# A gated recurrence and a max-out layer on one core: a new opening order, weights folded in one fused step, transposes in halves

## The chip, the core and the metric

The kernel runs on one core of a Trainium2 chip. A core has five engines that run their own instruction queues in order: TensorE (PE: matmuls and the loads of their weights, PEld), VectorE (DVE), ScalarE (ACT), GpSimd (POOL), and SyncE (SP), which here only issues DMAs. The metric is the device time of one execution in microseconds (us); less is better.

## What is computed

A recurrence over time in each of 256 channels for 4 sequences of 6144 tokens, then a layer with the larger of two products:

```
sig = 1.0 / (1.0 + np.exp(-f_logit))
f = lower_bound + (1.0 - lower_bound) * sig
i = 1.0 - f
for t in range(S):
    h = f[:, t] * h + i[:, t] * x[:, t]
    y[:, t] = h
...
h1 = y @ w1            # 256 x 1024
h2 = y @ w2            # 256 x 1024
out = np.maximum(h1, h2) @ w_out     # 1024 x 256
```

The kernel writes 1 - lower_bound as `om` and uses three rewritings. With u = sigmoid(-f_logit), the forget term is f = 1 - om*u and the input term is om*u*x; the factor om is left out of the scan's input v = u*x and put into the weights instead. The maximum becomes h1 + relu(h2 - h1), so the hidden layer needs only the folded weight wd = om*(w2 - w1), and the linear part y @ w1 @ w_out is folded into one 256 x 256 matrix, `w13`.

## The kernel before, in words

The 24576 tokens are cut into 48 blocks of 512 (`TB`), 12 to a sequence. Channels lie on the partitions in two halves of 128 (`KC`), hidden units in 8 groups of 128 (`FC`). For each block PE does 8 slots: in a slot, one hidden group (`hidden`, L253: two matmuls of 512 columns into a PSUM buffer `dT`, of which there are five) and one eighth of the output product of the block before (`project`, L305: five matmuls of 256 columns into `psO`, three buffers). ScalarE turns each `dT` into `rt` by a relu (L234); 24 such buffers hold three blocks' worth.

The first four blocks (`NP`) are the opening. Their inputs are loaded in natural order as f32, gated by ScalarE (`gate_nat`, L107), multiplied by VectorE (`drive_nat`, L112), turned by PE through an identity matrix (`turn_pe`, L120), and scanned by VectorE (`scan`, L142). In the same stretch the weights are loaded in quarters of 256 hidden units ("chunks" 0 to 3; chunk k holds hidden groups 2k and 2k+1) and prepared: `diff` (L378) computes w2 - w1 in f32, `scale` (L384) multiplies by `om` into bf16 `wd`; `round_w1` and `round_wout` cast to bf16; `turn_w1`, `keep_w1`, `linear_weights` and `keep_linear` build `w13`.

What runs in which order in the opening is written out by hand in two strings. `LOADS` (L445) is the order of SP's loads: f0a is the first half of block 0's f_logit, x0a that of x, w13 is chunk 3 of w1, w23 chunk 3 of w2, wo3 chunk 3 of w_out. `PLAN` (L449) is the order of work; each engine takes its own items from it in that order. A suffix .a, .v or .p names ScalarE, VectorE or GpSimd. G is a gate, V a drive, TU and TV the turns of u and v, F a forget, S a scan, RW and RO casts of w1 and w_out, D a difference, SC a scaling, TW a turn of w1, KW its copy out of PSUM, W13 a piece of the linear weights, KL its copy out, H a hidden half or group, R a relu, P an output step (P020: block 0, hidden group 2, first 256 tokens), L a linear step, O a copy out, warm n idle matmuls. CA starts the feed of the later blocks.

From block 4 on, GpSimd casts f_logit and x of two blocks at a time (`cast`, L167) into a bf16 scratch in DRAM, and SP brings them into SBUF transposed (`turn_dma`, L176). `cast_behind` (L182) lets GpSimd read one element of a landed transpose before it issues the next pair's casts. `gate_of` and `turn_of` (L546 to L549) say in which slot a block is gated and a pair is turned; a gated block runs `gate`, `drive`, and for each half a forget and a scan (L579 to L585). Results are copied out of `psO` and sent by SP (`send_out`, L319) in groups of 256 rows, eight buffers deep.

Of the kernel before, what the change touches and what calls it, by code (L numbers as in the profile page):

```python
# [9 lines left out]
BF16 = mybir.dt.bfloat16  # L10
ALU = mybir.AluOpType
AF = mybir.ActivationFunctionType
P = 128
# [3 lines left out]
def kernel(  # L17
# [36 lines left out]
    scratch = ctx.enter_context(  # L54
        tc.tile_pool(name="scratch", bufs=1, space=bass.MemoryType.DRAM)
    )
    ttpool = ctx.enter_context(tc.tile_pool(name="turned", bufs=3))
    midpool = ctx.enter_context(tc.tile_pool(name="mid", bufs=2))
    ypool = ctx.enter_context(tc.tile_pool(name="ypool", bufs=4))
    rpool = ctx.enter_context(tc.tile_pool(name="rpool", bufs=3 * FC))  # L60
# [113 lines left out]
            )  # L174

    def turn_dma(c):  # L176
        for s, name in enumerate(("fs", "xs")):
            t = ttpool.tile([P, KC, CB * TB], BF16, name=("fT", "xT")[s])
            turned[c, s] = t
            nc.sync.dma_start_transpose(out=t[:], in_=spare[c % NS, name][:])  # L180

    def cast_behind(c):  # L182

        if c + 1 < NCH:
            last = CB * TB - 1
            nc.gpsimd.tensor_copy(out=held[:], in_=turned[c, 0][:, KC - 1, last : last + 1])  # L186
            cast(c + 1)

    def part(j, s):
        c, o = divmod(j - NP, CB)  # L190
        return turned[c, s][:, :, o * TB : (o + 1) * TB]

    def gate(j):
        ffs[j] = midpool.tile([P, KC, TB], BF16, name="ff")
        ys[j] = ypool.tile([P, KC, TB], BF16, name="y")
        us[j] = midpool.tile([P, KC, TB], BF16, name="u")
        nc.scalar.activation(out=us[j][:], in_=part(j, 0), func=AF.Sigmoid, scale=-1.0)  # L197

    def drive(j):
        vs[j] = midpool.tile([P, KC, TB], BF16, name="v")  # L200
        nc.vector.tensor_tensor(out=vs[j][:], in0=us[j][:], in1=part(j, 1), op=ALU.mult)  # L201

    def forget_half(j, h, on_act=False):
        forget(ffs[j][:, h, :], us[j][:, h, :], h, on_act)
# [107 lines left out]
    def copy_out(j, g, on_act=False):  # L312
# [3 lines left out]
        else:  # L316
            nc.vector.tensor_copy(out=osbs[j, g][:], in_=pos[j, g, 0][:])  # L317

    def send_out(j, g):  # L319
        r0 = j * TB + 2 * g * P  # L320
        nc.sync.dma_start(
            out=out[r0 : r0 + 2 * P, :].rearrange("(p r) d -> p r d", r=2),
            in_=osbs[j, g][:],
        )

    def store(j, g):
        copy_out(j, g)
# [47 lines left out]
        )  # L375
        nc.vector.tensor_scalar_add(out=nom[:], in0=pt, scalar1=-1.0)

    def diff(k, h, eng):  # L378
        cols = slice(k * QF, (k + 1) * QF)
        eng.tensor_tensor(  # L380
            out=wdf[:, h, cols], in0=w2n[:, h, cols], in1=w1n[:, h, cols], op=ALU.subtract
        )

    def scale(k, h, on_dve):  # L384
        cols = slice(k * QF, (k + 1) * QF)
        o, i, m = wd[:, h, cols], wdf[:, h, cols], om[:, h : h + 1]
        if on_dve:
            nc.vector.tensor_scalar_mul(out=o, in0=i, scalar1=m)  # L388
        else:
            nc.scalar.activation(out=o, in_=i, func=AF.Copy, scale=m)  # L390

    def turn_w1(k):
        pts[k] = ps_d.tile([P, 2, D], BF16, name="dT")
# [49 lines left out]


    LOADS = """  # L445
    f0a x0a f0b w13 w23 x0b w12 w22 wo3 w10 w20 w11 wo2 w21 f1a x1a wo0 f1b x1b wo1
    f2a f2b x2a x2b f3 x3
    """
    PLAN = """  # L449
    G0a RW3.p keeps_T keeps V0a TU0a D31.p warm3 TV0a D30.p G0b F0a0.v warm4 TU0b  # L450
    D21.p F0a1.v S0a1 S0a0 V0b F0b1.a warm1 TW3 F0b0.a RW0.p warm5 TV0b RW2.v S0b1
    D01.p KW3.a TW2 SC31.a SC30.a KW2.a S0b0 RO3.a H06a H07a D20.v SC21.a warm3 H06b
    SC20.v H07b D00.v W133 RW1.v R07.a TW0 H04b H04a RO2.p H05a R06.a P071 SC00.v
    H05b P070 P061 D10.p TW1 SC01.a KW0.v R05.a R04.v H01a KW1.v H00a H00b H01b P040
    P050 P060 G1a P041 SC10.v V1a W132 R01.a D11.p TU1a RO0.p SC11.a P051 TV1a R00.a
    H02a F1a1.v F1a0.a RO1.p H03b S1a1 P011 G1b H02b S1a0 P010 H03a R02.a W130 V1b
    P001 R03.a TU1b H17a F1b1.v P000 TV1b H15a F1b0.a S1b1 S1b0 G2a H16a P031 P030
    P021 G2b W131 KL1.v TU2a F2a0.a P020 H17b H15b KL0.v H16b L01 L11 R17.a TU2b
    H10a H10b R16.a V2a R15.v F2a1.v H11b O01.a P161 H11a TV2a F2b0.a H12b P151 L10
    P171 V2b H12a R11.a F2b1.v R10.a S2a1 TV2b S2a0 G3b P150 R12.a S2b1 G3a L00 S2b0  # L460
    H13a V3b TU3b O00.a H13b P101 R13.a F3b1.v H14a P160 F3b0.v H14b P100 P170 H20
    H26 V3a TU3a P111 F3a1.v H21 R14.a H27 R20.a F3a0.v R26.a TV3a S3a1 P120 H24
    TV3b R21.a P121 P110 S3a0 H22 R27.a S3b1 P130 R24.a R22.a S3b0 H23 P131 R23.a
    H25 P140 O10.v P141 R25.a O11.v CA
    """

    engines = {"a": nc.scalar, "v": nc.vector, "p": nc.gpsimd}
# [18 lines left out]
    def issue(item):  # L486
        name, _, e = item.partition(".")
        eng, on_dve, on_act = engines.get(e), e == "v", e == "a"
        kind = name.rstrip("0123456789ab")
        arg = ["ab".index(c) if c in "ab" else int(c) for c in name[len(kind) :]]  # L490
        if kind == "warm":
            keep_warm(arg[0])
        elif name == "keeps_T":
            turn_bound()
        elif name == "keeps":
            keeps()
        elif kind in ("G", "V") and len(arg) == 2:
            (gate_nat if kind == "G" else drive_nat)(arg[0], 2 * arg[1], 2 * arg[1] + 2)
        elif kind in ("TU", "TV"):
            turn_pe(arg[0], "UV".index(kind[1]), arg[1])  # L500
        elif kind == "F" and len(arg) == 3:
            j, x, h = arg
            tok = slice(x * HB, (x + 1) * HB)
            forget(ffs[j][:, h, tok], uT[j, x][:, h, :], h, on_act)
        elif kind == "S" and len(arg) == 3:
            j, x, h = arg
            scan(j, h, x * HB, (x + 1) * HB, vT[j, x][:, h, :])
        elif kind == "RW":
            round_w1(arg[0], eng)
        elif kind == "RO":  # L510
            round_wout(arg[0], eng)
        elif kind == "D":
            diff(arg[0], arg[1], eng)
        elif kind == "SC":
            scale(arg[0], arg[1], on_dve)
        elif kind == "TW":
            turn_w1(arg[0])
        elif kind == "KW":
            keep_w1(arg[0], eng)
        elif kind == "W":  # L520
            linear_weights(int(name[3]))
        elif kind == "KL":
            keep_linear(arg[0], on_dve)
        elif kind == "H":
            (hidden_half if len(arg) == 3 else hidden_whole)(*arg)
        elif kind == "R":
            relu(arg[0], arg[1], on_dve)
        elif kind == "P":
            pair_steps(arg[0], arg[2], [arg[1]])
        elif kind == "L":  # L530
            pair_steps(arg[0], arg[1], [FC, FC + 1])
        elif kind == "O":
            copy_out(arg[0], arg[1], on_act)
            outs.append(arg)
            send_pending()
        elif kind == "CA":
            nc.gpsimd.tensor_copy(out=held[:], in_=ins[2][1][:, 3, D - 1 : D])
            cast(0)
            turn_dma(0)
            cast_behind(0)  # L540
            send_pending()
        else:
            raise ValueError(item)
# [7 lines left out]
    with tc.manual_schedule():  # L551
        for j in range(NP):
            alloc_in(j)
        nc.scalar.dma_start(out=lbr[:], in_=lower_bound.rearrange("(h p) -> h p", p=P))
        for name in LOADS.split():
            load_item(name)
        nc.vector.memset(warm[:], 0.0)  # L557
        make_identity(nc, ident[:])
        nc.vector.tensor_copy(out=ident_b[:], in_=ident[:])
        keep_warm(7)  # L560
        for item in PLAN.split():
            issue(item)
        assert not outs

        for j in range(3, NBLK + 1):
            for fc in range(FC):
                if j < NBLK:
                    hidden(j, fc)
                project(j - 1, fc)
                if fc == 0 and j > 3:  # L570
                    store(j - 2, 1)
                if fc == 4 and j < NBLK:
                    store(j - 1, 0)
                if j == NBLK and fc in (3, 5, 7):
                    if fc == 3:
                        store(j - 1, 0)
                    else:
                        store_row(j - 1, 1, (fc - 5) // 2)
                if (j, fc) in gate_of:  # L579
                    b = gate_of[j, fc]  # L580
                    gate(b)
                    drive(b)
                    for h in range(KC):
                        forget_half(b, h)
                        scan_half(b, h)  # L585
                if (j, fc) in turn_of:
                    turn_dma(turn_of[j, fc])
                    cast_behind(turn_of[j, fc])
# [30 lines left out]
```

## Time and profile before

| | |
|---|---|
| median of 7 runs | 397.62 us (397.07 to 397.79) |
| the profiled execution | 397.61 us, its span 395.8 us |
| mean granted TensorE clock | 0.999 |
| PE busy from 0 to 10 us | 8.17 of 10.00 us |
| PE busy from 10 to 20 us | 9.28 of 10.00 us |
| PE busy from 20 to 30 us | 10.00 of 10.00 us |
| PE busy from 100 to 200 us | 99.32 of 100.00 us |
| HBM over the span | 257 GB/s |

The span is the time from the first to the last instruction of the program in the profile; the execution's time has a little around it (397.61 against 395.8). A busy share is the time in which an engine works on at least one instruction. Some matmul records are missing from the trace, which shows as a small loss in busy time where there is none. Warm-up matmuls, whose results nobody reads, count as busy too, so a busy PE in the first 14 us isn't a useful PE.

Other rows of the profile that the opening touches, with shapes kept apart over the first 36 us (out<-in, shape, count, busy us, mean ns of one): the gate of 512 elements on ScalarE takes 626 ns, a forget of 256 elements 473 ns on ScalarE and 345 ns on VectorE, a scan of 256 elements 732 ns on VectorE, a relu of 512 elements 595 ns on ScalarE, a scaling of 256 elements 507 ns on ScalarE. In the steady part a gate of 1024 elements takes 1048 ns, a scan of 512 elements 1284 ns, a copy out of `psO` 679 ns.

### The profile page before, as it was taken

The page shows a single profiled execution, that of the slowest core. Times are in us where ns is not written, and L with a number is a line of the kernel's source. Part 1 is how long each engine was busy: PE and PEld are TensorE (multiplying, and loading weights), DVE is VectorE, ACT ScalarE, POOL GpSimd, SP SyncE. Part 2 cuts the span into 40 slices and gives each one's busy share as a digit, 9 for nine tenths or more (in the row PEclk, how much of TensorE's full clock was granted, in tenths as well). Part 3 has the DMA queues.
Part 4 walks back from the last instruction along what each step waited for, and adds up shares of the span by engine and source line. Part 5 has one row for each costly group of instructions (what it writes and reads, how often), then busy time and mean ns, then how long its engine had stood idle before and what let it go on. Part 6 is the DMA issues. An engine that isn't in the chain of part 4 may idle for free.

```text
span 395.8 us, 7146 instructions
## 1 busy us (share of the span) xinstructions
PE 387.8 (98%) x2793; PEld 275.0 (69%) x2840; DVE 251.8 (64%) x366; ACT 273.7 (69%) x451; POOL 36.9 (9%) x83
## 2 busy tenths in 40 slices
PE   8999999999999999999999999999999999999996
PEld 3796677777676777776767777767677777676775
DVE  3896965656755775576567656755775576567622
ACT  4787776677667666766676677667766766676661
POOL 2411011101101101101101001011011010100000
PEclk9999999999999999999999999999999999999999
DMA  7999999999999999999989999998998898981122
GB/s 241 350 247 186 237 213 214 235 218 215 237 199 196 236 207 222 193 228 201 209 193 196 198 206 198 221 216 184 205 208 208 186 192 206 214 188 53 55 81 107
DMA packets 125079, 79.12 MB, mean 200 GB/s; under 512 B 94195, under 2 KB 101621, under 8 KB 125045
## 3 DMA queue, kind: packets, MB, share of 16 engines
q1 hardware_dynamic: 113072, 55.59, 57.3%
q0 software_dynamic: 11968, 23.07, 35.4%
q8 instruction: 22, 0.36, 0.4%
q14 instruction: 13, 0.10, 0.1%
q10 hardware_dynamic: 4, 0.00, 0.0%
HBM read 53.48 MB, written 48.23 MB: 257 GB/s over the span
## 4 chain that ended last, share of the span: by engine, by line
PE 95%; DMA 1%; DVE 1%; issue 1%; SPq 1%; DVEq 0%
PE psO L268 53%; PE dT L245 39%; PE dT L225 2%; DMA xn<-in_x_dram 1%; PE dT L126 1%; SPq L100 0%; PE psO L413 0%; DVE vn L113 0%; SPq L344 0%; DVE y L149 0%; DVE wdf L380 0%; DVE wd L388 0%; DVE row L332 0%; PE dT L396 0%; DVEq L113 0%
## 5 line engine op out<-in xcount | busy, mean ns | idle before, releaser
L240 ACT ACTIVATE rt<-dT 128x512 bf16<-128x512 f32 x382 | 223.5, 596 | 106.4 <-PE dT L245 102.9
L268 PE MATMUL psO<-wob,rt 128*128 128x256 bf16 x1536 | 231.0, 273 | 0.2
L268 PEld LDWEIGHTS <-rt 128*128 128x128 bf16 x1536 | 150.0, 98 | 94.6
L245 PE MATMUL dT<-y,wd 128*128 128x512 bf16 x690 | 208.8, 379 | 2.2
L149 DVE TENSOR_TENSOR_SCAN y<-ff,y,v 128x512 bf16<-128x512 bf16 x82 | 105.3, 1284 | 2.9
L317 DVE COPY osb<-psO 128x512 f32<-128x512 f32 x93 | 62.8, 679 | 68.2 <-PE psO L268 68.2
L245 PEld LDWEIGHTS <-wd 128*128 128x128 bf16 x736 | 72.0, 98 | 8.8
L268 PE MATMUL psO<-w,y 128*128 128x256 bf16 x384 | 72.4, 273 | 0.0
L201 DVE TENSOR_TENSOR v<-u,xT 128x1024 bf16<-128x1024 bf16 x44 | 30.5, 693 | 59.6 <-ACT u L197 53.0
L197 ACT ACTIVATE u<-fT 128x1024 bf16<-128x1024 bf16 x44 | 46.1, 1048 | 0.5 <-DMA fT<-fs 0.5
L268 PEld LDWEIGHTS <-y 128*128 128x128 bf16 x384 | 37.6, 98 | 4.4
L186 POOL CAST held<-fT 128x1 f32<-128x1 bf16 x21 | 4.6, 218 | 280.7 <-DMA fT<-fs 280.7
L138 DVE TENSOR_SCALAR ff<-u,nom 128x512 bf16<-128x512 bf16 x88 | 29.8, 338 | 0.0
L170 POOL DMA_DIRECT2D fs<-in_f_logit_dram x22 | 12.3, 560 | 5.1 <-issue 5.0
L170 POOL DMA_DIRECT2D xs<-in_x_dram x22 | 12.1, 551 | 0.0
L149 DVE TENSOR_TENSOR_SCAN y<-nff,y,dT 128x256 bf16<-128x256 bf16 x14 | 9.6, 732 | 1.8 <-PE dT L126 1.3
L225 PE MATMUL dT<-y,wd 128*128 128x256 bf16 x64 | 10.1, 273 | 0.3 <-DVE wd L388 0.2
L433 PE MATMUL psO<-warm 128*128 128x512 bf16 x22 | 7.9, 493 | 1.2 <-DVE warm L557 1.2
L149 DVE TENSOR_TENSOR_SCAN y<-ff,v 128x512 bf16<-128x512 bf16 x6 | 7.3, 1225 | 0.2
L108 ACT ACTIVATE un<-fn 128x512 bf16<-128x512 f32 x8 | 4.9, 626 | 3.2 <-DMA fn<-in_f_logit_dram 3.1
L113 DVE TENSOR_TENSOR vn<-un,xn 128x512 bf16<-128x512 bf16 x8 | 6.1, 766 | 1.2 <-DMA xn<-in_x_dram 1.2
L225 PEld LDWEIGHTS <-wd 128*128 128x128 bf16 x64 | 5.8, 98 | 1.4 <-DVE wd L388 0.4
(40 smaller groups left out, 52.1 us busy)
## 6 DMA issues: line engine op xcount, KB each, us to landing
out_dram<-osb SPq DMA_DIRECT2D x95, 256.0 KB, 3.1
fs<-in_f_logit_dram POOLq DMA_DIRECT2D x22, 512.0 KB, 6.8
xs<-in_x_dram POOLq DMA_DIRECT2D x22, 512.0 KB, 9.5
fn<-in_f_logit_dram SPq DMA_DIRECT2D x6, 256.0 KB, 6.0
xn<-in_x_dram SPq DMA_DIRECT2D x6, 256.0 KB, 5.8
w1n<-in_moe_w_dram SPq DMA_DIRECT2D x4, 256.0 KB, 6.0
w2n<-in_moe_w_dram SPq DMA_DIRECT2D x4, 256.0 KB, 6.0
won<-in_moe_w_out_dram SPq DMA_DIRECT2D x4, 256.0 KB, 6.0
```

Source lines behind the costliest of these rows:

```text
L113: nc.vector.tensor_tensor(out=vs[j][:, q0:q1, :], in0=us[j][:, q0:q1, :], in1=ins[j][1][:, q0:q1, :], op=ALU.mult,)
L138: nc.vector.tensor_scalar(out=o, in0=i, scalar1=nom[:, h : h + 1], scalar2=1.0, op0=ALU.mult, op1=ALU.add)
L149: nc.vector.tensor_tensor_scan(out=ys[j][:, h, t0:t1], data0=ffs[j][:, h, t0:t1], data1=v, initial=initial, op0=ALU.mult, op1=ALU.add,)
L170: nc.gpsimd.dma_start(out=spare[c % NS, name][:], in_=src[b, k * TB : (k + CB) * TB, :], max_dma_last_dim=4096,)
L197: nc.scalar.activation(out=us[j][:], in_=part(j, 0), func=AF.Sigmoid, scale=-1.0)
L201: nc.vector.tensor_tensor(out=vs[j][:], in0=us[j][:], in1=part(j, 1), op=ALU.mult)
L225: nc.tensor.matmul(dts[j, fc][:, tok], lhsT=wd[:, kc, unit(fc)], rhs=ys[j][:, kc, tok], start=(first and kc == 0), stop=(not first and kc ...
L240: nc.scalar.activation(out=rt[:], in_=dts[j, fc][:], func=AF.Relu)
L245: nc.tensor.matmul(dts[j, fc][:], lhsT=wd[:, kc, unit(fc)], rhs=ys[j][:, kc, :], start=(kc == 0), stop=(kc == KC - 1),)
L268: nc.tensor.matmul(ps, lhsT=lhsT, rhs=rhs, start=start, stop=stop, skip_group_check=True)
L317: nc.vector.tensor_copy(out=osbs[j, g][:], in_=pos[j, g, 0][:])
L433: nc.tensor.matmul(idle[:].rearrange("p r d -> p (r d)"), lhsT=warm[:, 0:P], rhs=warm[:], start=True, stop=True,)
```

## The change

It has five parts.

1. The weights are folded in another form. `diff` and `scale` go; `fold_w1` (plan item A) computes om*w1 into `wdf` on GpSimd, ScalarE or VectorE, and `fold_diff` (item B) computes om*w2 - wdf on VectorE in one operation. Before, there were 8 differences and 8 scalings; after, 8 A (6 on GpSimd, one each on ScalarE and VectorE) and 8 B.
2. `LOADS` and `PLAN` are new. Block 0's x moves ahead of the weights, chunk 1 is the first to be used (H03, H02), then chunks 3, 2 and 0. The warm matmuls are 26 in place of 23.
3. `CA` waits for an element of block 2's f_logit in place of its x; with the new load order that is the load before.
4. `turn_dma` issues four transposes of one block each (f, x, f, x) in place of two of two blocks; the buffers are twice as many and half as large. `send_out` sends blocks 45 and 46 in two halves of a group each.
5. In the loop a gated block does both forgets before the drive; block 4's forgets go to ScalarE.

The diff, without what only follows from names:

```diff
-    ttpool = ctx.enter_context(tc.tile_pool(name="turned", bufs=3))
+    ttpool = ctx.enter_context(tc.tile_pool(name="turned", bufs=6))
...
     def turn_dma(c):
-        for s, name in enumerate(("fs", "xs")):
-            t = ttpool.tile([P, KC, CB * TB], BF16, name=("fT", "xT")[s])
-            turned[c, s] = t
-            nc.sync.dma_start_transpose(out=t[:], in_=spare[c % NS, name][:])
+        b0, n = NP + c * CB, CB
+        for o in range(n):
+            for s, name in enumerate(("fs", "xs")):
+                t = ttpool.tile([P, KC, TB], BF16, name=("fT", "xT")[s])
+                turned[b0 + o, s] = t
+                nc.sync.dma_start_transpose(
+                    out=t[:], in_=spare[c % NS, name][o * TB : (o + 1) * TB, :]
+                )
...
-            last = CB * TB - 1
-            nc.gpsimd.tensor_copy(out=held[:], in_=turned[c, 0][:, KC - 1, last : last + 1])
+            b0, n = NP + c * CB, CB
+            nc.gpsimd.tensor_copy(out=held[:], in_=turned[b0, n - 1][:, KC - 1, TB - 1 : TB])
             cast(c + 1)
...
     def send_out(j, g):
+        if NBLK - 4 < j < NBLK - 1:
+            for r in range(2):
+                nc.sync.dma_start(out=rows_out(j, g)[:, r, :], in_=osbs[j, g][:, r, :])
+        else:
+            nc.sync.dma_start(out=rows_out(j, g), in_=osbs[j, g][:])
...
-    def diff(k, h, eng):
-        eng.tensor_tensor(
-            out=wdf[:, h, cols], in0=w2n[:, h, cols], in1=w1n[:, h, cols], op=ALU.subtract
-        )
+    def fold_w1(k, h, eng):
+        o, i, m = wdf[:, h, cols], w1n[:, h, cols], om[:, h : h + 1]
+        if eng is nc.scalar:
+            nc.scalar.activation(out=o, in_=i, func=AF.Copy, scale=m)
+        else:
+            eng.tensor_scalar_mul(out=o, in0=i, scalar1=m)
...
-    def scale(k, h, on_dve):
-        o, i, m = wd[:, h, cols], wdf[:, h, cols], om[:, h : h + 1]
-        if on_dve:
-            nc.vector.tensor_scalar_mul(out=o, in0=i, scalar1=m)
-        else:
-            nc.scalar.activation(out=o, in_=i, func=AF.Copy, scale=m)
+    def fold_diff(k, h):
+        nc.vector.scalar_tensor_tensor(
+            out=wd[:, h, cols],
+            in0=w2n[:, h, cols],
+            scalar=om[:, h : h + 1],
+            in1=wdf[:, h, cols],
+            op0=ALU.mult,
+            op1=ALU.subtract,
+        )
...
     LOADS = """
-    f0a x0a f0b w13 w23 x0b w12 w22 wo3 w10 w20 w11 wo2 w21 f1a x1a wo0 f1b x1b wo1
-    f2a f2b x2a x2b f3 x3
+    f0a x0a f0b x0b w12 w11 w13 w21 wo1 w23 w22 wo3 f1a w10 w20 x1a f1b wo2 x1b wo0
+    f2a x2a f2b x2b f3 x3
     """
     PLAN = """
-    G0a RW3.p keeps_T keeps V0a TU0a D31.p warm3 TV0a D30.p G0b F0a0.v warm4 TU0b
-    D21.p F0a1.v S0a1 S0a0 V0b F0b1.a warm1 TW3 F0b0.a RW0.p warm5 TV0b RW2.v S0b1
-    D01.p KW3.a TW2 SC31.a SC30.a KW2.a S0b0 RO3.a H06a H07a D20.v SC21.a warm3 H06b
-    SC20.v H07b D00.v W133 RW1.v R07.a TW0 H04b H04a RO2.p H05a R06.a P071 SC00.v
+    G0a V0a keeps_T TU0a warm1 TV0a keeps A20.p F0a1.a S0a1 G0b RW1.p F0a0.a warm7
+    TU0b V0b F0b0.a S0a0 A11.p warm2 TV0b F0b1.a RW2.a A31.p A10.a S0b0 S0b1 B10 B11
+    warm4 TW2 TW1 RW3.a KW1.a warm2 TW3 RO1.a A21.v A30.p warm3 H03a H02a H03b B31
+    B30 KW2.a KW3.v B21 B20 H02b RO3.p W131 H06a R02.a H06b A00.p R06.v R03.a RW0.v
+    H07a P020 P021 H07b G1a W133 H05a H05b R07.a P061 A01.p H04a R05.a H04b B00 TW0
+    TU1a RO2.p B01 V1a P070 P030 H00a R04.a F1a1.v H01b H01a KW0.a TV1a P031 P060
...
         elif kind == "CA":
-            nc.gpsimd.tensor_copy(out=held[:], in_=ins[2][1][:, 3, D - 1 : D])
+            nc.gpsimd.tensor_copy(out=held[:], in_=ins[2][0][:, 3, D - 1 : D])
...
                     gate(b)
+                    for h in range(KC):
+                        forget_half(b, h, b == NP)
                     drive(b)
                     for h in range(KC):
-                        forget_half(b, h)
                         scan_half(b, h)
```

## The prediction

> **What bounds the kernel now.** I read the page's busy shares first, then the chain that ended last, then the chain in order of time over the first 45 us, SP's issues, and last the groups of the opening with shapes kept apart.
>
> ```profile
> PE 387.8 (98%) x2793; PEld 275.0 (69%) x2840; DVE 251.8 (64%) x366; ACT 273.7 (69%) x451; POOL 36.9 (9%) x83
> PE 95%; DMA 1%; DVE 1%; issue 1%; SPq 1%; DVEq 0%
> ```
>
> PE is busy 98% of the span and 95% of the chain. The chain in order of time (start, length, what) shows where the other 5% lie:
>
> ```profile
> 3.28 5.68 DMA xn<-in_x_dram
> ...
> 9.06 1.21 DVE vn L113
> ...
> 12.20 0.75 DVE wdf L380
> ...
> 12.97 0.72 DVE wd L388
> ...
> 13.74 0.83 PE dT L225 x6
> ...
> 41.78 0.55 PE psO L268 x5
> 42.33 0.43 PE dT L245 x2
> 42.76 0.55 PE psO L268 x5
> ```
>
> Until 13.74 us the chain runs over a load and VectorE; from 13.74 it is PE alone. From 41.78 a slot (two 128x512 and five 128x256 matmuls) takes 42.76 - 41.78 = 0.978 us, so a block of 8 slots takes 7.82 us; the same row stands at 374.13 us, 340 slots of 0.9775 later. So there is nothing to win or lose between 13.74 us and the end unless a new stall is made; the kernel's time is PE's useful work plus what PE loses before 13.74.
>
> That loss is a ledger. Useful matmuls before 13.74: 28 transposes at 0.054 us (four take 0.22 in the chain) = 1.5, and 12 of 256 columns at 0.109 = 1.3. Lost: 13.74 - 2.8 = 10.9 us. The rest is warm-up matmuls and waits.
>
> SP has eight DMA semaphores in turn, so from load 11 on it issues load n+8 when load n has landed (start, length):
>
> ```profile
> 6.28 0.43 SPq L344 DMA_DIRECT2D w2n<-in_moe_w_dram  x1
> 7.53 0.37 SPq L344 DMA_DIRECT2D w1n<-in_moe_w_dram  x1
> 8.25 0.37 SPq L349 DMA_DIRECT2D won<-in_moe_w_out_dram  x1
> 8.98 0.37 SPq L344 DMA_DIRECT2D w2n<-in_moe_w_dram  x1
> 9.75 0.37 SPq L100 DMA_DIRECT2D fn<-in_f_logit_dram  x1
> 10.50 0.37 SPq L100 DMA_DIRECT2D xn<-in_x_dram  x1
> 11.25 0.37 SPq L349 DMA_DIRECT2D won<-in_moe_w_out_dram  x1
> 12.01 0.37 SPq L100 DMA_DIRECT2D fn<-in_f_logit_dram  x1
> ```
>
> These are landings of places 3 to 10: 6.28, 7.53, 8.25, 8.98, 9.75, 10.50, 11.25, 12.01, then one each 0.75 us. All these loads are 256 KB, so I keep the places and put the new order into them.
>
> ```profile
> L380 POOL TENSOR_TENSOR wdf<-w2n,w1n 128x256 f32<-128x256 f32 x6 | 4.3, 726 | 1.3 <-DMA w2n<-in_moe_w_dram 1.2
> L388 DVE TENSOR_SCALAR wd<-wdf,om 128x256 bf16<-128x256 f32 x3 | 2.0, 652 | 0.0
> L355 POOL CAST w1b<-w1n 128x512 bf16<-128x512 f32 x2 | 1.2, 614 | 7.0 <-DMA w1n<-in_moe_w_dram 7.0
> ```
>
> The second number is the mean of one in ns: prices of the operations that go or that resemble the new ones.
>
> **What the skill says.** SBUF — State Buffer, section Who interferes with whom: a VectorE operation with two SBUF inputs, or in a two-port mode, and a GpSimd operation that reads SBUF exclude each other for the whole instruction. The trace agrees: L388 took 0.46 us on one occasion and 0.72 and 0.78 beside GpSimd work; the drive product (L113) took 0.68 alone, and 1.20 when it began at 9.06 with GpSimd's L380 running to 9.72. GPSIMD Engine Reference, section 3.1: 2.6 cycles per element with two inputs, 1.03 for short bodies bound by one port. The trace fits: 256 elements with two inputs 0.726 us, a 512-element cast 0.614. TensorE: Matmul & The Clock Gate, Part 1: the array starts at half rate and is freed after about 3.4 us of work. Here warm-up matmuls are 0.43 us apart until about 6.2 us and 0.217 after.
>
> **The change, part by part.**
>
> *Weight folding.* Before, a 256-column half cost a difference (0.726 on GpSimd, 0.41 undisturbed on VectorE), which needs w1 and w2, then a scaling. Now A = om*w1 needs w1 alone and is ready early; after w2 lands only B is left, one fused VectorE operation with two f32 SBUF inputs. The trace shows neither. B: nearest row VectorE's L380, 0.41 us, 0.34 start to start; bounds 0.38 and 0.55; I take 0.41. A on GpSimd: the cast leaves 0.614 - 512*1.03/1200 = 0.17 fixed, so 0.17 + 256*1.03/1200 = 0.39 below; above, the two-input 0.73; I take 0.45.
>
> *New load order*, by place: x0b 4 (7.53), w12 5, w11 6 (8.98), w13 7 (9.75), w21 8 (10.50), wo1 9 (11.25), w23 10 (12.01), w22 11 (12.76), wo3 12 (13.51), w10 14, w20 15 (15.8).
>
> *The walk to the first hidden matmul (H03a).* VectorE, in its order: V0b at 7.57 takes 0.68, then three scans (0.73 each, 0.66 to 0.73 apart): y of block 0 complete at 10.3. Then B10 at 10.52 (w21 plus a signal), B11 at 10.86, done 11.30. GpSimd has A11 done near 10.1 (after RW1, 9.01 to 9.62), ScalarE A10 at 9.84: both ready. PE meanwhile: TW3 waits for ScalarE's cast of w13 (9.77 to 10.40), then three warm matmuls, 10.66 to 11.31. Both chains meet: H03a at 11.33. Useful by then: the 28 transposes, 1.5. Lost: 9.8.
>
> *After it.* H03, H02 in halves (4 x 0.217) and W131 (0.43) fill PE to 12.65. H06a needs B31 and B30, which start at 12.05 when w23 is there and end at 12.79: hole 0.2. Then H06, H07a, P020, P021, H07b fill to 14.15. W133 needs wo3's cast on GpSimd: lands 13.51, GpSimd waits for B20's port to 13.83, cast done 14.34: hole 0.24. Chunk 0 (w20 at 15.8) is wanted at about 16.8 and ready then. Later the two engines that feed PE have no queue longer than its stock. Lost in all 9.8 + 0.2 + 0.24 + 0.05 small ones = 10.3, against 10.9: **gain 0.6 us**.
>
> *Cast gate.* The first casts wait for f2b at place 23 instead of x2b at 24: about 0.75 us sooner. They meet the last loads f3, x3: up to about 1 us later, and G3a stands early in ScalarE's queue (about 25.1 against a landing of 24.6). Relus behind it have half a microsecond or more of stock. I take 0; a wait over 1.5 us would cost up to 0.9.
>
> *Block 4's forget on ScalarE.* Before, its gate ran from 38.46 (1.05 us), its VectorE work ended at 43.38, its first use was at 44.1. Now two 512-wide activations, 0.47 + 256*0.83/1000 = 0.69 each, run beside the drive, and VectorE loses 0.68. ScalarE is late by 1.05 + 1.3 = 2.3 us; relus take 0.60 of each 0.978 slot and five dT buffers hold some 3.9 us. No stall; without that cover about 1 us.
>
> *Transposes halved* (88 for 44 on SP, order f, x, f, x), turned buffers doubled. The next cast now waits for the x of the pair's first block: the second index of `turned` is the stream. Cycle: cast to landing of xs 9.5 (the median), half a transpose about 1.0 to 1.7 and 2.2 to land, 0.5 of issue: 13.2 to 13.9 us, against 13.2 to 14.3 between the issues of casts 3 to 6 (50.64, 64.89, 78.35, 91.59 us) and 15.64 that PE takes for two blocks. From block 12 on f has landed at least 5 us before its gate (90.77 against 96.13), so 0; SP's outs behind a transpose have eight buffers.
>
> *Outputs of blocks 45, 46 in two*: four more SP issues of 0.33 us at a time when SP waits; the last output stays where it was. *Forgets before the drive*: same VectorE sum. Both 0.
>
> Sum against the profiled execution, 397.61 us (span 395.8): 397.0. The median is 397.62, so no correction.
>
> **Rivals.** *Larger gain*: the two holes and the start all hang on landings of w21, w23, wo3. Should these come 0.25 us earlier, the start and both holes shrink: gain 1.1, 396.5. For it: places are a steady 0.75 us apart. Against: the bytes ahead of them are the same. *No gain*: y of block 0 ends only 0.2 us before B10. If x0b takes 0.4 us longer in place 4 (place 3 was 2.1 us after place 2, which I can't explain), or the clock stays half past 8.5 us so that the seven warm matmuls hold TU0b back, H03a comes 0.5 later: 397.5. *Slower, by GpSimd*: A11, A31, A30 stand behind one another, and B waits for each as well as for its port. At 0.45 they end at 11.0 with a microsecond to spare; each 0.1 us above about 0.55 moves start and H06a together. Break-even is near 0.8 us, above the two-input row; at 1.0 us H03a begins 0.6 later and H06a's hole and chunk 0 lose as much again: 398.8. For it: a pointer scalar in software is unpriced. Against: one stream should not cost more than two. *Starved feed*: halved transposes costing as much as whole ones, and casts slowed with them, past 15.64 us a pair; each 0.3 us over, times 20 pairs, is 6 us: about 403.
>
> **How the numbers follow.** A measurement of this kernel tells about 0.2%, 0.8 us, from no change. Forecast near 397.0 (396.8 to 397.4): 0.50, no measurable change. Larger gain 0.24: faster. No gain 0.10: within. GpSimd 0.10 and feed 0.06: slower. So faster 0.24, within 0.60, slower 0.16. The range leaves out the feed, half of the GpSimd case and the largest gains: 396.3 to 398.2.
>
> **What would show it.** The first L225 row near 11.3, a wait of 0.2 before the next pair of L225, a L424 matmul waiting for GpSimd's wob near 14.4, then PE alone at 0.978 a slot; block 4 with no gap. Wrong: A on GpSimd over 0.6 us, B over 0.5, y of block 0 after 10.5, or any PE gap past 20 us.

## The result, and the profile after

| | before | after |
|---|---|---|
| median of all runs shown | 397.48 us (396.54 to 398.08, 31 runs) | 402.2 us (397.86 to 406.65, 13 runs) |
| ratio after : before | | 1.0096, interval 1.0076 to 1.0115 |
| span of the profiled execution | 395.8 us | 400.4 us |
| mean cycle from one pair's casts to the next, from the second casts on | 15.11 us | 15.95 us |

The changed kernel is slower by about 1%. Its runs also spread over 9 us, those of the kernel before over 1.5 us. The ratio leaves out the runs that lie more than 1.5% above the fastest; for this kernel they showed the same TensorE clock as the others, so the spread is its own, and the ratio of the plain medians (402.2 / 397.48 = 1.012) is as fair a number.

The page of the changed kernel: busy shares, shares of the chain that ended last, the row of DMA load (tenths, 40 slices), groups (busy us, mean ns | idle before, released by), and the DMA issues with their median us to landing. The two rows of the kernel before that they are compared with follow.

```profile
PE 390.6 (98%) x2796; PEld 274.2 (68%) x2843; DVE 247.3 (62%) x363; ACT 272.5 (68%) x456; POOL 44.0 (11%) x81
DMA  7999999989999999989999999999999999999523
PE 67%; DMA 24%; ACT 4%; issue 2%; DVE 2%; SPq 1%; POOL 1%; ACTq 0%; POOLq 0%; DVEq 0%
L197 ACT ACTIVATE u<-fT 128x1024 bf16<-128x1024 bf16 x44 | 46.3, 1052 | 31.1 <-DMA fT<-fs 31.0
L201 DVE TENSOR_TENSOR v<-u,xT 128x1024 bf16<-128x1024 bf16 x44 | 30.3, 688 | 17.6 <-DMA xT<-xs 15.6
fs<-in_f_logit_dram POOLq DMA_DIRECT2D x22, 512.0 KB, 7.7
xs<-in_x_dram POOLq DMA_DIRECT2D x22, 512.0 KB, 11.0
```

```profile
L197 ACT ACTIVATE u<-fT 128x1024 bf16<-128x1024 bf16 x44 | 46.1, 1048 | 0.5 <-DMA fT<-fs 0.5
xs<-in_x_dram POOLq DMA_DIRECT2D x22, 512.0 KB, 9.5
```

PE's share of busy time is 98% as before and tells nothing. The chain does: PE holds 67% of it where it held 95%, and DMA 24% where it held 1%. The gates of the steady part (L197) waited 31.0 us for the transposed f_logit; in the kernel before they waited 0.5 us. The second cast of a pair (xs) lands 11.0 us after its issue, before 9.5.

Where the time goes is read from the first output step of each block (my own reading of PE's timeline). Block 3's stands at 44.35 us (before 44.55), block 20's at 177.29 (before 177.49): in this pair of traces the opening won 0.2 us, and 17 blocks later nothing was lost. Block 24's stands at 210.41 (before 208.77), and PE ends at 397.29 (before 392.73). The loss is 4.77 us in stretches near 178, 195, 211, 259, 306, 322 and 339 us. The first of them in the chain in order of time (start, length, what):

```profile
172.57 0.42 PE psO L268 x4
172.99 4.25 DMA fT<-fs
...
177.35 1.06 ACT u L197
178.41 1.47 ACT rt L240 x3
...
179.92 0.50 PE psO L268 x3
```

The transpose of the pair's first f lands late, the gate starts late at 177.35, three relus stand behind it in ScalarE's queue, and PE waits for the last of them. The forecast of 397.0, no change, was wrong; what came resembles its "starved feed" rival (about 403), to which it gave 0.06.

Around this stretch, SP's transposes and GpSimd's casts in the changed kernel, and then SP's transposes of the same pair in the kernel before (start, length of the issue, what, and in brackets the idle time before):

```profile
172.99 1.23 SPq L182 DMA_TRANSPOSE fT<-fs  x1
176.22 1.23 SPq L182 DMA_TRANSPOSE xT<-xs  x1
177.54 1.25 SPq L182 DMA_TRANSPOSE fT<-fs  x1
178.84 1.29 SPq L182 DMA_TRANSPOSE xT<-xs  x1
```

```profile
162.51 0.64 POOL L190 CAST held<-xT 128x1 f32<-128x1 bf16 x1 [14.13 <-DMA xT<-xs]
163.08 0.55 POOL L170 DMA_DIRECT2D fs<-in_f_logit_dram  x1
163.62 0.55 POOL L170 DMA_DIRECT2D xs<-in_x_dram  x1
179.73 0.64 POOL L190 CAST held<-xT 128x1 f32<-128x1 bf16 x1 [15.55 <-DMA xT<-xs]
180.30 0.55 POOL L170 DMA_DIRECT2D fs<-in_f_logit_dram  x1
```

```profile
158.93 3.84 SPq L180 DMA_TRANSPOSE fT<-fs  x1
162.85 2.12 SPq L180 DMA_TRANSPOSE xT<-xs  x1
```

In the changed kernel fs of this pair landed at 172.94, and SP issued the first f at once. It was done issuing at 174.22, and the second f, whose data were there, could have followed. But SP issues in order, and the next in the queue was the first x, which waits for xs: that landed at 176.16. So the second f went out at 177.54, 3.3 us later than its data allowed. It and the second x were then still to be moved when the next casts went out at 180.30. From casts to casts this pair took 17.2 us; PE uses a pair up in 15.64. So what comes late is the next pair, its first f with it: all the gates that waited were those of the first block of a pair.

### The profile page after: what moved, and what is told of

The parts are those of the page before. It is cut to its first block, busy times and chain, and to the rows that moved or that the text cites. A ratio compares the mean times of both kernels' runs of the same rounds, so it can differ in the third digit from the quotient of the medians.

```text
span 400.4 us, 7198 instructions
## 1 busy us (share of the span) xinstructions
PE 390.6 (98%) x2796; PEld 274.2 (68%) x2843; DVE 247.3 (62%) x363; ACT 272.5 (68%) x456; POOL 44.0 (11%) x81
## 4 chain that ended last, share of the span: by engine, by line
PE 67%; DMA 24%; ACT 4%; issue 2%; DVE 2%; SPq 1%; POOL 1%; ACTq 0%; POOLq 0%; DVEq 0%
PE psO L268 38%; PE dT L245 28%; DMA fT<-fs 9%; DMA xs<-in_x_dram 8%; ACT rt L240 3%; DMA xT<-xs 3%; ACT u L197 2%; DMA fn<-in_f_logit_dram 2%; DMA w2n<-in_moe_w_dram 1%; DMA w1n<-in_moe_w_dram 1%; DVE y L149 1%; SPq L100 0%; POOL fs L170 0%; DVE v L201 0%; DVE osb L317 0%
## 5 line engine op out<-in xcount | busy, mean ns | idle before, releaser
L240 ACT ACTIVATE rt<-dT 128x512 bf16<-128x512 f32 x379 | 215.7, 596 | 83.5 <-PE dT L245 80.2
L149 DVE TENSOR_TENSOR_SCAN y<-ff,y,v 128x512 bf16<-128x512 bf16 x82 | 100.9, 1272 | 1.5
L317 DVE COPY osb<-psO 128x512 f32<-128x512 f32 x92 | 60.6, 677 | 42.4 <-PE psO L268 42.2
L138 DVE TENSOR_SCALAR ff<-u,nom 128x512 bf16<-128x512 bf16 x86 | 26.5, 350 | 78.1 <-ACT u L197 77.9
L197 ACT ACTIVATE u<-fT 128x1024 bf16<-128x1024 bf16 x44 | 46.3, 1052 | 31.1 <-DMA fT<-fs 31.0
L190 POOL CAST held<-xT 128x1 f32<-128x1 bf16 x21 | 12.5, 596 | 297.1 <-DMA xT<-xs 297.1
```

Of the source, the lines that this page charges most:

```text
L138: nc.vector.tensor_scalar(out=o, in0=i, scalar1=nom[:, h : h + 1], scalar2=1.0, op0=ALU.mult, op1=ALU.add)
L149: nc.vector.tensor_tensor_scan(out=ys[j][:, h, t0:t1], data0=ffs[j][:, h, t0:t1], data1=v, initial=initial, op0=ALU.mult, op1=ALU.add,)
L190: nc.gpsimd.tensor_copy(out=held[:], in_=turned[b0, n - 1][:, KC - 1, TB - 1 : TB])
L197: nc.scalar.activation(out=us[j][:], in_=turned[j, 0][:], func=AF.Sigmoid, scale=-1.0)
L240: nc.scalar.activation(out=rt[:], in_=dts[j, fc][:], func=AF.Relu)
```

## The experiments

I began with another theory (the "wait theory"): the element of x that GpSimd reads before the next casts (`turned[b0, n - 1]`, an x because n - 1 is 1) is what makes the cycle long. Its rival put the loss on the rest of the change.

**Casts that wait for f.** The changed kernel with one index changed:

```diff
-            nc.gpsimd.tensor_copy(out=held[:], in_=turned[b0, n - 1][:, KC - 1, TB - 1 : TB])
+            nc.gpsimd.tensor_copy(out=held[:], in_=turned[b0, 0][:, KC - 1, TB - 1 : TB])
```

> The changed kernel with one index altered: the next pair's casts wait for f of the pair's first block, no longer for its x. Wait theory (the casts hang on the landing of xs, so a pair's cycle is 15.9 us against the 15.64 us that PE takes for two blocks): casts about 13 us apart when nothing else holds them, no idle time of ScalarE before the gates beyond 1 us, 397.3 us (before less 0.2 us from the opening). Split theory (halved transposes are slow in themselves): 401 us or more, casts still about 16 us apart.

Measured: 424.15 us (420.24 to 433.03), ratio 1.0643 (1.058 to 1.0706). The cycle grew to 16.65 us, xs took 11.56 us to land. SP in this run:

```profile
178.62 3.00 SPq L182 DMA_TRANSPOSE fT<-fs  x1
181.71 4.00 SPq L182 DMA_TRANSPOSE xT<-xs  x1
185.80 1.25 SPq L182 DMA_TRANSPOSE fT<-fs  x1
187.11 1.29 SPq L182 DMA_TRANSPOSE xT<-xs  x1
```

The casts now come sooner, and three half transposes instead of two run beside them. Two of the four issues here take 3.0 and 4.0 us instead of 1.25, and the x issued at 187.11 landed only at 197.06. The wait theory is refuted: waiting less makes it worse. (From block 3 on PE loses 22.1 us in this run. PE waited up to 3.75 us at a stretch, and in three spells of 13.65 us in all the granted clock was 0.5, which is at most 6.8 of the 22.1.)

**The two halves of the change.** Three kernels: the changed kernel with the old feed (`turn_dma`, `cast_behind` and the three whole buffers of before), the kernel before with its casts waiting for x instead of f, and the kernel before with the new feed alone. The edits, each against the kernel named:

```diff
 # changed kernel, old feed (the kernel before with the new feed is the reverse)
-        for o in range(n):
-            for s, name in enumerate(("fs", "xs")):
-                t = ttpool.tile([P, KC, TB], BF16, name=("fT", "xT")[s])
...
+        for s, name in enumerate(("fs", "xs")):
+            t = ttpool.tile([P, KC, CB * TB], BF16, name=("fT", "xT")[s])
...
 # kernel before, casts wait for x
-            nc.gpsimd.tensor_copy(out=held[:], in_=turned[c, 0][:, KC - 1, last : last + 1])
+            nc.gpsimd.tensor_copy(out=held[:], in_=turned[c, 1][:, KC - 1, last : last + 1])
```

> The changed kernel with the feed of before (whole pairs transposed at once, casts waiting for f of the pair); opening, weight folding, block 4's forget and split outputs stay changed. Wait and split theories both: 397.3 us. Plan theory (the new opening leaves the feed late for good): 400 us or more.

> The kernel before with only the wait moved: casts wait for x of the whole pair in place of f, transposes stay whole. Wait theory: cycle 9.5 to 11 us to the landing of xs, 2.1 us for the transpose, 2.3 us to land and 0.5 us more, so 14.4 to 15.9 us, at the edge: 398 to 402 us. Split theory: 397.5 us, as before.

> The kernel before with only the changed feed (four half transposes f, x, f, x, casts waiting for the first block's x). Wait and split theories: 401 to 404 us, like the changed kernel. Plan theory: 397.5 us.

Measured:

| kernel | us | ratio (interval) | cycle, us | xs landing, us |
|---|---|---|---|---|
| changed, old feed | 397.94 | 1.0019 (1.001 to 1.0028) | 15.10 | |
| before, casts wait for x | 397.35 | 1.0001 (0.9991 to 1.001) | 15.19 | 8.77 |
| before, new feed | 408.77 | 1.0323 (1.027 to 1.0376) | 16.24 | 10.64 |

The loss lies in the feed alone; everything else in the change together costs 0.2% (the interval ends at 0.28%). Waiting for x costs nothing by itself when the transposes are whole. Why the new feed costs more in the kernel before than in the changed one isn't settled.

**An overlap theory, and its failure.** Next I held that the cost is the overlap: transposes that run beside the next casts lengthen these. Then casts that wait for later halves should mend it, and whole transposes left beside the casts should starve the kernel before. The edits are again the one index: `turned[b0 + 1, 0]` (the second f) and `turned[b0 + 1, 1]` (the last half) in the changed kernel; in the kernel before, `turned[max(c - 1, 0), min(c, 1)]`, so that a cast waits for the x of the pair before and goes out beside all transposes of the present one.

> The changed kernel, casts waiting for f of the pair's second block, so one half transpose (x of the second block) is left to run beside the next casts, not two. Overlap theory (transposes that run beside casts make the 16 DMA engines slower; the changed wait lets more of them do so): 397.5 to 399 us, mean time of a 256-byte packet near 23 ns. Halving theory (four transposes cost the DMA engines more than two, wherever they run): 401 us or more. The old wait theory (a longer chain is slower): 410 us or more.

> The changed kernel, casts waiting for the last transpose of the pair, so nothing overlaps. Overlap theory: fs and xs land sooner (5.5 and 8.8 us), the chain is 8.8 + 3.9 + 2.2 + 0.5 = 15.4 us, 397.5 to 400 us. Halving theory: 401 us or more. Wait theory: 415 us or more.

> The kernel before with whole transposes, casts waiting for x of the pair before the one that is turned, so casts may run beside both transposes. Overlap theory: 402 us or more, mean time of a 256-byte packet over 28 ns. Halving theory: 397.5 us or a little less, since casts start sooner.

Measured: waiting for the second f 404.11 us, ratio 1.0127 (1.0052 to 1.0202), cycle 16.14; waiting for the last half 405.31, ratio 1.0198 (1.0146 to 1.025), cycle 16.11. In the last one nothing is left beside the casts, and they do land sooner (fs 5.94, xs 8.51 us), but the cycle isn't shorter. The whole overlap in the kernel before gave 402.66, ratio 1.0141 (1.0109 to 1.0174), a time near what the theory asked for; yet its trace shows one loss of 6.45 us, between the first output steps of blocks 4 and 5, after two pairs' casts had gone out 2.0 us apart, and none later. Of this one, PE's wait is 3.38 us; the granted clock was 0.5 for 6.83 us from 54.79 on, which accounts for most of the rest. Nor did the DMA packets get much slower: those of 256 bytes took 23.7 ns on average, where over 28 was expected and the kernel before has 22.8. So overlap as such doesn't cost a steady amount, and the theory falls.

**The order in SP's queue.** What the first two of these kernels share with the changed one is f, x, f, x. The next kernel is the changed one with the loops exchanged, so that SP issues f, f, x, x, and casts that wait for the second f:

```diff
-        for o in range(n):
-            for s, name in enumerate(("fs", "xs")):
+        for s, name in enumerate(("fs", "xs")):
+            for o in range(n):
...
-            nc.gpsimd.tensor_copy(out=held[:], in_=turned[b0, n - 1][:, KC - 1, TB - 1 : TB])
+            nc.gpsimd.tensor_copy(out=held[:], in_=turned[b0 + 1, 0][:, KC - 1, TB - 1 : TB])
```

> The changed kernel with halves in the order f, f, x, x and casts waiting for the second f: the order and wait of before, only cut in halves. Overlap theory: two halves of x stay beside the next casts as in the kernel before, 397.9 us like the changed kernel with the old feed. Halving theory: 401 us or more.

Measured: 397.76 us, ratio 1.0007 (1.0 to 1.0015), cycle 15.11. The loss is gone. SP and GpSimd of this kernel (SP's lines join two halves, "x2"):

```profile
161.90 3.73 SPq L182 DMA_TRANSPOSE fT<-fs  x2
165.72 2.60 SPq L182 DMA_TRANSPOSE xT<-xs  x2
...
177.07 3.64 SPq L182 DMA_TRANSPOSE fT<-fs  x2
```

```profile
168.05 0.18 POOL L190 CAST held<-fT 128x1 f32<-128x1 bf16 x1 [12.11 <-DMA fT<-fs]
168.56 0.55 POOL L170 DMA_DIRECT2D fs<-in_f_logit_dram  x1 [0.32 <-issue]
...
183.22 0.18 POOL L190 CAST held<-fT 128x1 f32<-128x1 bf16 x1 [13.58 <-DMA fT<-fs]
183.73 0.55 POOL L170 DMA_DIRECT2D fs<-in_f_logit_dram  x1 [0.32 <-issue]
```

Both f halves go out together while xs is still being cast, and the x halves follow: casts to casts 183.73 - 168.56 = 15.17 us, with four halves as in the changed kernel. No gate of this kernel waited for f. Engine by engine in stretches (us, then busy us and count of PE, PEld, DVE, ACT, POOL, then PE's clock, DMA share, GB/s; the share sums the packets' times over the 16 DMA engines and can pass 1), first the changed kernel, then this one:

```profile
100.00:200.00 100.00, 98.25 (x693) 68.63 (x704) 63.25 (x89) 68.62 (x113) 11.39 (x21) 1.00 0.97 195
200.00:300.00 100.00, 98.84 (x698) 69.21 (x709) 63.43 (x90) 68.69 (x115) 9.99 (x18) 1.00 1.00 203
```

```profile
100.00:200.00 100.00, 100.00 (x719) 70.14 (x718) 62.63 (x91) 71.09 (x116) 10.18 (x21) 1.00 1.11 206
200.00:300.00 100.00, 100.00 (x718) 70.02 (x717) 63.64 (x90) 70.33 (x116) 8.61 (x19) 1.00 1.11 204
```

The kernel that isn't starved moves as much or more: 206 and 204 GB/s against 195 and 203. So the changed kernel isn't short of bandwidth. The DMA share says less, since the kernel before, which isn't starved either, has 1.06 and 0.96 in these stretches.

**Order against wait, and order without halves.** Two things were changed at once, so three more kernels: the same order f, f, x, x with the wait of the changed kernel put back (`turned[b0, n - 1]`); the kernel before with whole transposes in the order x, f, its casts still waiting for f; and the kernel before with halves in the order f, f, x, x.

```diff
 # kernel before, whole transposes, x first
-        for s, name in enumerate(("fs", "xs")):
+        for s, name in ((1, "xs"), (0, "fs")):
```

> The f, f, x, x kernel with the casts waiting for x of the first block again, the wait of the changed kernel. Order theory (it is the second f, queued on SP behind an x that waits for xs, that lengthens a pair's cycle, and not what the casts wait for): 397.8 us, cycle 15.6 us or less. If the wait for x is what costs: 401 us or more.

> The kernel before, whole transposes, with SP's order turned round: x first, then f, casts waiting for f. Nothing is cut in halves. Order theory: f can't start before xs has landed; cycle 8.8 to 11 us to xs, two transposes of 2.2 us, 2.3 us to land, 0.5 us: 16 to 18 us against 15.64, so 405 us or more. If halves are needed for the loss: 397.5 us.

> The kernel before with halves in the order f, f, x, x, casts waiting for the second f; opening as before. Order theory: 397.5 us, as before: halves cost nothing by themselves. Halving theory: 399 us or more.

| kernel | us | ratio (interval) | cycle, us |
|---|---|---|---|
| changed, f, f, x, x, old wait | 397.81 | 1.0004 (0.9996 to 1.0013) | 15.18 |
| before, whole, x then f | 409.31 | 1.0286 (1.0254 to 1.0319) | 16.10 |
| before, halves f, f, x, x | 397.55 | 0.9998 (0.9989 to 1.0007) | 15.07 |

With f, f, x, x the wait makes no difference, halving makes none, and exchanging the order alone takes the changed kernel from 402.2 to 397.81 us. (With f, x, f, x the wait does matter: the four that were run gave 402 to 424 us, but none is free of the loss.) Whole transposes with x ahead of f starve the kernel before too. Its SP and its waits (waited for: us in total, times, longest):

```profile
159.28 2.08 SPq L180 DMA_TRANSPOSE xT<-xs  x1
161.53 2.84 SPq L180 DMA_TRANSPOSE fT<-fs  x1
164.46 2.02 SPq L321 DMA_DIRECT2D out_dram<-osb  x4
175.59 2.12 SPq L180 DMA_TRANSPOSE xT<-xs  x1
177.88 1.94 SPq L180 DMA_TRANSPOSE fT<-fs  x1
```

```profile
ACT u L197 <- DMA fT<-fs: 39.2, 20, 5.2
PEld L268 <- ACT rt L240: 12.8, 21, 3.8
```

f goes out directly behind x, only once xs has landed, and the gates wait 39.2 us for it. The sizes aren't to be compared with those of the halves: of the 13.25 us that PE loses here from block 3 on, 6.8 come at once between blocks 4 and 5 (a wait of 3.44 us, then a granted clock of 0.5 for 6.83 us), and the other 6.4 after block 22, in stretches as in the changed kernel.

**A quicker opening on top.** The f, f, x, x kernel with two A moved from GpSimd to ScalarE, to win the opening's gain:

```diff
-    warm4 TW2 TW1 RW3.a KW1.a warm2 TW3 RO1.a A21.v A30.p warm3 H03a H02a H03b B31
+    warm4 TW2 TW1 RW3.a KW1.a warm2 TW3 RO1.a A30.a A21.v warm3 H03a H02a H03b B31
...
-    H07a P020 P021 H07b G1a W133 H05a H05b R07.a P061 A01.p H04a R05.a H04b B00 TW0
+    H07a P020 P021 H07b G1a W133 H05a H05b R07.a A01.a P061 H04a R05.a H04b B00 TW0
```

> The f, f, x, x kernel with two of the six A on GpSimd (A30 and A01) moved to ScalarE, behind the cast RO1 and the relu R07. Opening theory (A takes 0.955 us on GpSimd and leaves the holes of 0.41 us near 12.7 and 0.35 us near 16.9 on PE): holes of 0.2 us and 0, block 3's first output step 0.5 us earlier, 397.2 us. If something else sets these holes: 397.8 us, as with f, f, x, x alone.

Measured: 397.19 us, ratio 0.9994 (0.9986 to 1.0002). The first hole in PE is 0.09 us, the second 0.28, against 0.41 and 0.35 in the changed kernel. It has the lowest median of all that were run, and can't be told from the kernel before.

## Why the prediction was wrong, by its own steps

**The feed's cycle: the step that failed.** "Cycle: cast to landing of xs 9.5 ..., half a transpose about 1.0 to 1.7 and 2.2 to land, 0.5 of issue: 13.2 to 13.9 us ... so 0." The cycle splits at the issue of the first x. From the casts to that issue the changed kernel takes 11.69 us on average over 19 pairs, where the step had 9.5; from there to the next casts 4.28 us, where the step's other terms give 3.7 to 4.4. So the x half and the issue were priced right, and the whole miss of 2.2 us lies in the first part. Of it 0.54 us are the time between the issues of fs and xs: the 9.5 was counted from xs's own issue, and the sum leaves this out. The rest is the landing of xs, 11.1 us on average over these pairs. The term that moved was the one taken over from the old trace and costed as if the change didn't touch it. It moved because of the order in SP's queue, a fact that the prediction had in hand ("order f, x, f, x") and didn't follow: it priced each transpose and never asked which of them was ready and stood behind one that wasn't. Before, all of f was transposed while xs was being cast; after, half of f waits for xs. That this order is the cause is shown by exchanging it alone, in both directions: f, f, x, x with the old wait takes the loss away, x ahead of f brings one into the kernel before.

How the order lengthens the cycle is in part argued. With the same wait for the first x, the order f, x, f, x leaves two halves to run beside the next casts and f, f, x, x leaves one; xs then lands after 11.0 and 9.4 us (medians). Over the kernels with halves the landing follows that count: 8.5 us with none left (casts that wait for the last half), 9.4 with one, 10.4 to 11.0 with two, 11.6 with three (casts that wait for the first f). But a late xs alone doesn't starve anything: the f, f, x, x kernel whose casts wait for the second f has 10.9 us too and loses nothing, since its f halves and its next casts don't stand behind xs. And with none left the casts start later instead, and the cycle is no better (16.11 us): with f, x, f, x, three halves lie behind the landing of xs whatever the casts wait for.

**The slack it compared with: right.** The step held 13.2 to 14.3 us, the cycles of casts 3 to 6, against PE's 15.64. In the kernel before the ten cycles from the second casts on take 14.50 us on average, the ten after these 15.72: by then the feed has caught up and goes at PE's pace, because SP's transposes stand behind results that are still to be computed and sent. The waits of SP show it (waited for: us in total, times, longest), first before, then after:

```profile
SPq L321 <- DVE osb L317: 188.0, 72, 5.8
SPq L180 <- DMA fs<-in_f_logit_dram: 18.9, 7, 9.6
```

```profile
SPq L182 <- DMA fs<-in_f_logit_dram: 122.0, 22, 10.1
SPq L182 <- DMA xs<-in_x_dram: 52.8, 22, 3.7
SPq L328 <- DVE osb L317: 17.7, 8, 5.2
```

So the 15.11 us of the first table mixes two stretches, and the feed's slack was about 1.1 us a pair. In the changed kernel SP waits for casts to the end, and its ten cycles take 15.99 and then 15.91 us: it loses 0.3 us a pair on PE instead. In the kernel before, the first f of the eleventh pair lands 10.8 us ahead of its gate; in the changed one, from the second pair on, each of these gates starts 0.1 us after its f lands.

That also says why nothing is seen until block 20. I compared these 21 gates with the same gates of the kernel before, less the 0.2 us of the opening and with PE's earlier losses added. They are 0.1 to 3.3 us late. The 14 that are at most 1.71 us late cost PE nothing, and the seven that are at least 2.08 us late cost it their lateness less 1.83 us; block 22's is the first of them (3.27 us late, 1.45 us lost). So PE has 1.83 us in hand before each of these gates. So close to the threshold a small difference between runs decides how often PE waits, which would account for the spread from 397.9 to 406.7; that is argued, not tested.

**The rival "starved feed".** Right in size (403, measured 402.2) and in that the casts land later, wrong in cause: it blamed the price of halves. Halves are free, as the kernel before with f, f, x, x shows. Its 0.3 us a pair was assumed and not worked out, so that the size fits is luck.

**A on GpSimd.** Taken at 0.45 us, bounds 0.39 and 0.73. Rows of the changed kernel's first 36 us, with shapes apart:

```profile
L389 POOL TENSOR_SCALAR wdf<-w1n,om 128x256 f32<-128x256 f32 x6 | 5.7, 955 | 7.9 <-DVE vn L113 6.9 <-DMA w1n<-in_moe_w_dram 0.9
L394 DVE SCALAR_TENSOR_TENSOR wd<-w2n,om,wdf 128x256 bf16<-128x256 f32 x8 | 4.6, 591 | 0.9 <-POOL wdf L389 0.7 <-DMA w2n<-in_moe_w_dram 0.2
```

A took 0.955 us, more than the two-input difference it replaces (0.726); the assumption that one input stream can't cost more than two was false. The Trainium skill's GPSIMD Engine Reference, section 3.1, from which the lower bound came, gives 1.03 cycles per element for short bodies that are bound by the read and write ports; this operation doesn't keep to it. B averaged 0.591, against 0.41 taken and 0.55 as the upper bound; alone it took 0.48 to 0.49, beside GpSimd's work up to 0.88. PE's timeline of the opening:

```profile
11.32 1.16 PE L225 MATMUL dT<-y,wd 128*128 128x256 bf16 x8
12.32 0.60 PE L424 MATMUL psO<-wob,w1T 128*128 128x256 bf16 x4
13.16 0.83 PE L225 MATMUL dT<-y,wd 128*128 128x256 bf16 x6 [0.24 <-DVE wd L394]
...
16.89 0.27 PE L225 MATMUL dT<-y,wd 128*128 128x256 bf16 x1
17.35 0.72 PE L225 MATMUL dT<-y,wd 128*128 128x256 bf16 x5 [0.19 <-DVE wd L394]
```

The first hidden matmul came at 11.32 where the walk had 11.33. The hole behind it was 0.41 us instead of 0.2, because B30 waited for GpSimd's A30 and not for w23; a second one of 0.35 us stands before 17.35, where B01 waited for A01. Together that is 0.76 against the 0.44 of the step. Of the two holes in the step the second, before W133, didn't come: wo3's cast ran from 13.34 to 13.95, and PE went on at 14.48 without a gap. (The step gave that cast 0.51 us, where the row that it shows has 0.614.)

**The gain of 0.6 us: not there.** In this trace block 3 began 0.2 us sooner than before, not 0.6, and even the sign isn't firm: block 3's first step lay between 43.5 and 44.6 us in six traces with the old opening (43.9 on average; the trace that the ledger was made from is the latest of them), and between 44.25 and 45.1 in seven with the new one (44.7 on average). One run each can't settle the size, but it points to a later start. The changed kernel with the old feed is slower by 0.4 to 1.1 us, the one with f, f, x, x by 0 to 0.6; and in the traces of both, PE takes 348.2 us from block 3's first step to its end, as in the kernel before. So what they lose is lost in the opening, or, for at most 0.3 us in the first of them, after PE's end. The rival "slower, by GpSimd" had the price nearly right (1.0) and its effect, 1.2 us, somewhat too large: in the trace of the changed kernel A11 and A10 were early enough at that price too. The run with two A moved to ScalarE (397.19 us, against 397.76 without that) fits the view that A's price is what the opening loses, but the parts of the opening weren't taken apart further.

**The rest.** Block 4's forgets on ScalarE (0.714 us each, 0.69 taken), the forgets ahead of the drive, the cast gate and the split outputs were each costed at 0. No gap in blocks 4 to 20 contradicts it (7.82 us a block, as before); the split outputs lie outside these blocks and weren't tested apart.

## What to carry to other kernels

In an in-order queue the order is part of the price: for each issue that is moved or split, ask when its data are ready and what it now stands behind. A feed that runs beside the bound engine has a cycle of its own; work out its slack from a stretch in which nothing but its own chain holds it, since a feed that has caught up goes at the bound engine's pace and its mean hides the slack. Distrust a term taken from the old trace if the change alters what runs beside it. When a loss sets in late and comes in scattered stretches, find out how late an arrival may be before the bound engine waits. And don't read half a microsecond of gain from one pair of traces, if the same code starts a block up to a microsecond apart in others.

## What the runs showed of the hardware

- A GpSimd multiplication of 256 f32 by a value per partition took 0.955 us, where a difference of two such inputs took 0.726 and a cast of 512 elements 0.614.
- B, a VectorE operation with two SBUF inputs, took 0.54 us when it began at 11.87 and 0.69 when it began at 15.91, both times with GpSimd's A at work throughout, and 0.48 to 0.49 alone. By the Trainium skill, SBUF — State Buffer, section Who interferes with whom, the two would exclude each other for the whole instruction. Here the first ended at 12.41 and the second at 16.60, before A did (about 12.58 and 16.78): slowed at most by 0.2 us, and not held until A's end. The spans on GpSimd are rough.
- A transpose issued just before or beside casts to DRAM can land 10 to 13 us after its issue (187.11 to 197.06 in the kernel whose casts wait for the first f), where 3.4 us is the median of the x halves in the changed kernel. That one landed in the same moment as fs of those casts. This was seen in the trace and not tested apart.
- In three runs (casts that wait for the first f; whole transposes left beside the casts; x ahead of f) PE waited 3.24 to 3.75 us at a stretch, four times in all, and 1.81 us once. With each of these waits came a spell of 3.41 or 6.83 us in which the granted clock was 0.5. In the other runs PE waited at most 1.53 us at a stretch after the first 20 us, and no such spell came from there to PE's end.
